# A dense SiLU layer on one core: the first two transposed tiles loaded by two transposes instead of one, and the loads behind them in another order

## The chip, the cores and the metric

The kernel runs on one core of a Trainium2 chip. The metric is the device time of one execution in microseconds (us); less is better. A core has TensorE (matrix products), ScalarE (activations), VectorE, GpSimd and SyncE (SP), each with an instruction stream of its own. SP and ScalarE also issue DMA transfers, and all transfers share the core's 16 DMA engines. Engines wait for each other and for transfers by semaphores.

## The reference

```
B, S, D, F = 1, 2048, 640, 1728            # all bfloat16
h   = einsum("bsd,df->bsf", x, w1)         # 2048 x 640 times 640 x 1728
h   = silu(h)
out = einsum("bsf,fd->bsd", h, w2)         # 2048 x 1728 times 1728 x 640
```

## The kernel before

The first product is computed transposed: `hT` holds the 1728 hidden features on partitions and the 2048 tokens along the free dimension. For that, `x` must be in SBUF with its 640 features on partitions, as five tiles of 128 (`xT[:, k, :]`, k = 0 to 4). The DMA engines transpose `x` on the way in (`turned`, line 90, and line 163). `w1` is kept as `w1s[:, k, :]`, 128 features of tile k by 1728 columns. The hidden features are cut into 13 tiles of 128 columns and a tail of 64. Tokens go in four chunks of 512.

A *step* (line 183) multiplies one 128 x 128 piece of `w1s` with one 128 x 512 piece of `xT`, as two matmuls on the two halves of the array's columns, into one PSUM bank. Elsewhere in the kernel the five steps of a hidden tile stand together. The opening of the first 512 tokens is different, because nothing has been loaded yet: it runs tile by tile over the features. `opening` (line 197) takes k = 0 for the first eight hidden tiles (eight PSUM banks), then k = 1 for the same eight (`sweep`, line 192), then k = 2 and 3; k = 4 follows at line 208 and ends the eight sums, which ScalarE then passes through SiLU (line 179) into `hT`. So each sweep of eight steps needs one *slab* `w1s[:, k, 0:1024]` (256 KB, `slab`, line 118) and one transposed tile `xT[:, k, 0:512]`. Then come the remaining five hidden tiles of the first tokens (lines 222 to 228, which need `ld_rest` and `ld_rest2`), then the three other chunks of tokens (line 229), each after its five transposes `ld_xc[c]`.

The order in which things are loaded is written out by hand. `early` (line 98) moves an instruction into the program's first block, ahead of the barrier that ends it; calls for one engine keep their order. SP's queue in that block is, before:

1. tiles 0 and 1 of the first 512 tokens, one transpose (line 123);
2. the last three hidden tiles of slab 0 (line 148, 96 KB);
3. slab 1, slab 2 (lines 149, 150);
4. tile 2 (line 151), slab 3 (152), tiles 3 and 4 in one transpose (153), slab 4 (154);
5. the columns of `w1` from 1024 on in two loads (lines 156 and 157).

Behind the barrier SP issues the fifteen transposes of the other chunks (line 163) and the loads of `w2` (lines 168 to 171). ScalarE issues one load, the first five hidden tiles of slab 0 (line 124, 160 KB; `NA` = 5), then loads its activation table (line 144).

While the first transfers are under way TensorE multiplies zeros (`dummies`, line 129): thirteen matmuls of 256 columns and a half-width pair (lines 137 and 138). It then waits for tiles 0 and 1 and for ScalarE's part of slab 0 (line 199), and from hidden tile `NA` on for SP's part (line 202).

The second product, from line 247 on, runs after all of this; the change does not touch it. It reads `w2s` and `hT`, and writes the output in blocks of 128 tokens.

Of the kernel before, what the change touches and what calls it, by code (L numbers as in the profile page):

```python
# [9 lines left out]
def bass_standalone__dense_activation_silu__prompt_kernel(  # L10
# [13 lines left out]
    P = 128  # L24
    NB = 8
    BANK = 512
    DT = D // P
    FT = F // P
    FL = F - FT * P
    SCH = 512  # L30
# [10 lines left out]
    with ExitStack() as es:  # L41
# [18 lines left out]
        def sem(name):  # L60
            s = es.enter_context(nc.semaphore(name))
            count[s.name if hasattr(s, "name") else name] = 0
            return [s, 0]

        def tick(ins, s, n=1):
            ins.then_inc(s[0], n)
            s[1] += n
            return (s, s[1])

        def wait(eng, *points):  # L70
            for pt in points:
                if pt is None:
                    continue
                s, v = pt
                key = (id(eng), id(s))
                if seen.get(key, 0) < v:
                    eng.wait_ge(s[0], v)
                    seen[key] = v
# [6 lines left out]
        def load(eng, out_ap, in_ap):  # L85
            s = sem(f"s_ld{n_dma[0]}")
            n_dma[0] += 1
            return tick(eng.dma_start(out=out_ap, in_=in_ap), s, 16)

        def turned(c0, c1, k0, k1):  # L90
            s = sem(f"s_tr{n_dma[0]}")
            n_dma[0] += 1
            return tick(sp.dma_start_transpose(
                out=xT[:, k0:k1, c0:c1], in_=xf[c0:c1, k0 * P:k1 * P]), s, 16)

        ET = mybir.EngineType

        def early(emit, engine, arrived=True):
            n = len(nc.main_func.blocks[0].instructions)
            r = emit()  # L100
            lst = nc.main_func.blocks[0].instructions
            new = lst[n:]
            del lst[n:]
            at = next(
                i for i, ins in enumerate(lst)
                if ins.opcode == ("EventSemaphore" if arrived else "Drain") and ins.engine == engine
            )
            lst[at:at] = new
            return r
# [2 lines left out]
        w2_v = w2[0:F0, :].rearrange("(ft p) d -> p ft d", p=P)  # L112

        NO = NB
        NA = 5
        CO = NO * P

        def slab(eng, k, f0=0, f1=NO):
            return load(eng, w1s[:, k, f0 * P:f1 * P], w1_v[:, k, f0 * P:f1 * P])

        ld_w1 = {}
        ld_t = {}
        ld_t[0] = ld_t[1] = early(lambda: turned(0, SCH, 0, 2), ET.SP, False)
        ld_w1[0] = early(lambda: slab(act, 0, 0, NA), ET.Activation, False)
        p_z = early(lambda: tick(dve.memset(z[:, :], 0.0), s_dve), ET.DVE, False)  # L125

# [2 lines left out]
        def dummies(n, w):  # L129
            for _ in range(n):  # L130
                for c0 in range(0, P, w):
                    pe.matmul(ps[c0:c0 + w, 3, 0:HB], lhsT=z[:, 0:w], rhs=z[:, :],  # L132
                              start=True, stop=True)

        def first_dummies():
            wait(pe, p_z)
            dummies(13, P)
            dummies(1, HC)

        p_warm = early(lambda: tick(pool.memset(warm[:, :], 0.0), s_pool), ET.Pool, False)  # L140
# [4 lines left out]

        early(warm_up, ET.Activation, False)

        ld_w1b = early(lambda: slab(sp, 0, NA, NO), ET.SP, False)
        ld_w1[1] = early(lambda: slab(sp, 1), ET.SP, False)
        ld_w1[2] = early(lambda: slab(sp, 2), ET.SP, False)  # L150
        ld_t[2] = early(lambda: turned(0, SCH, 2, 3), ET.SP, False)
        ld_w1[3] = early(lambda: slab(sp, 3), ET.SP, False)
        ld_t[3] = ld_t[4] = early(lambda: turned(0, SCH, 3, DT), ET.SP, False)
        ld_w1[4] = early(lambda: slab(sp, 4), ET.SP, False)
        CM = CO + 2 * P
        ld_rest = early(lambda: load(sp, w1s[:, :, CO:CM], w1_v[:, :, CO:CM]), ET.SP, False)
# [40 lines left out]
        def opening():  # L197
            first_dummies()
            wait(pe, ld_t[0], ld_w1[0])
            for ft in range(NO):  # L200
                if ft == NA:
                    wait(pe, ld_w1b)
                part(0, ft, 0, SCH, start=True)
            for k in range(1, DT - 1):
                sweep(k, 0, SCH, ld_w1[k], ld_t[k])
# [202 lines left out]
```

## Time and profile before

| | |
|---|---|
| three runs, us | 124.97, 124.90, 124.26; median 124.9 |
| profiled execution, span from first to last instruction | 123.8 us (the page gives no other time for it) |
| TensorE busy | 121.3 us, 98% of the span, 1056 matmuls |
| ScalarE busy | 38.8 us, 31% |
| VectorE busy | 6.9 us, 6% |
| bytes moved | 10.42 MB in 19625 packets |
| SP's DMA issues in the opening | 10, from 0 to 7.7 us |

The span counts from the first instruction that the page counts, here SP's first transpose, to the last. In the timeline each line has the start, the duration, the engine (SPq and ACTq are the DMA issues of SP and ScalarE: the duration is the time that the issue holds the queue, not the transfer), the line of the kernel, the operation, what it writes and reads, how many instructions are merged, and in brackets the idle time before and what ended it. PE is TensorE's matmul, PEld its weight load, which runs ahead of the matmul. The lists of DMA issues have the size and the median time from issue to landing.

### The profile page before, as it was taken

The numbers are of one execution on the slowest core, as the hardware profiler recorded it, in microseconds if no ns is written. First come the engines' busy times: TensorE is split into PE (matmuls) and PEld (weight loads), VectorE is DVE, ScalarE is ACT, GpSimd is POOL, SyncE is SP. The second block draws the span as 40 slices with busy tenths as digits, with TensorE's granted clock in tenths as the row PEclk, the third lists the DMA queues.
The fourth block names the chain that finished last, engine by engine and source line by source line (L and its number), as shares of the span: only waits on it lengthen the run. The fifth ranks groups of instructions, "written<-read, shape, count | busy, mean of one in ns | idle before, by whom it ended". The sixth has DMA issues, their size and how long they took to land.

```text
span 123.8 us, 2298 instructions
## 1 busy us (share of the span) xinstructions
PE 121.3 (98%) x1056; PEld 58.9 (48%) x1057; DVE 6.9 (6%) x11; ACT 38.8 (31%) x67; POOL 0.3 (0%) x5
## 2 busy tenths in 40 slices
PE   8999999999999999999999999999999999999993
PEld 5345545545545545545544444444444444444452
DVE  0000000000000000000000022002200300222001
ACT  4000985555555555555530011001100200110110
POOL 0000000000000000000000000000000000000000
DMA  6999974554894000000000004302200220023112
GB/s 138 239 246 331 138 86 91 100 77 107 214 394 157 0 0 0 3 5 0 0 0 5 0 0 101 74 0 105 107 0 5 106 106 0 5 106 116 53 66 82
DMA packets 19625, 10.42 MB, mean 84 GB/s; under 512 B 13728, under 2 KB 19104, under 8 KB 19616
## 3 DMA queue, kind: packets, MB, share of 16 engines
q1 hardware_dynamic: 19472, 10.11, 34.1%
q10 hardware_dynamic: 144, 0.16, 0.6%
q8 instruction: 8, 0.13, 0.5%
q14 instruction: 1, 0.01, 0.0%
HBM read 4.51 MB, written 2.62 MB: 58 GB/s over the span
## 4 chain that ended last, share of the span: by engine, by line
PE 95%; DMA 3%; ACT 0%; issue 0%
PE ps L175 95%; DMA xT<-in_x_dram 3%; ACT o_sb L256 0%
## 5 line engine op out<-in xcount | busy, mean ns | idle before, releaser
L175 PE MATMUL ps<-xT,w1s 128*64 128x512 bf16 x540 | 59.6, 384 | 0.1
L175 PE MATMUL ps<-w2s,hT 64*128 64x512 bf16 (+3 forms) x376 | 46.0, 369 | 0.2 <-issue 0.2
L175 PEld LDWEIGHTS ps<-xT,w1s 128*64 128x64 bf16 x540 | 30.0, 111 | 29.6 <-issue 1.2
L179 ACT ACTIVATE hT<-ps 128x512 bf16<-128x512 f32 x52 | 30.0, 607 | 29.9 <-PE ps L175 29.9
L175 PEld LDWEIGHTS ps<-w2s,hT 64*128 64x128 bf16 (+1 forms) x377 | 21.0, 95 | 24.2 <-issue 0.2
L256 ACT CAST o_sb<-ps 128x512 bf16<-128x512 f32 (+1 forms) x9 | 5.0, 551 | 41.5 <-PE ps L175 41.5
L175 PE MATMUL ps<-hT,w2s 64*128 64x512 bf16 x104 | 11.7, 376 | 0.0
L175 PEld LDWEIGHTS ps<-hT,w2s 64*128 64x128 bf16 x104 | 5.0, 94 | 6.3 <-issue 0.4
L254 DVE CAST o_sb<-ps 128x512 bf16<-128x512 f32 (+1 forms) x8 | 5.4, 675 | 40.5 <-PE ps L175 40.5
L254 DVE CAST oT<-ps 128x512 bf16<-128x512 f32 x2 | 1.4, 692 | 74.2 <-PE ps L175 74.2
L256 ACT CAST oT<-ps 128x512 bf16<-128x512 f32 x2 | 1.2, 586 | 10.6 <-PE ps L175 10.6
L132 PE MATMUL ps<-z 128*128 128x256 bf16 (+1 forms) x15 | 3.3, 419 | 0.4 <-DVE z L125 0.4
L175 PE MATMUL ps<-w2t,hTt 64*128 64x512 bf16 (+2 forms) x17 | 2.9, 363 | 0.0
L132 PEld LDWEIGHTS ps<-z 128*128 128x128 bf16 (+1 forms) x15 | 1.9, 142 | 1.5 <-issue 0.4
L179 ACT ACTIVATE hTt<-ps 128x512 bf16<-128x512 f32 x2 | 1.2, 598 | 1.0 <-PE ps L175 1.0
L144 ACT ACT_TABLE_LOAD x1 | 1.3, 1283 | 0.5 <-issue 0.5
L175 PEld LDWEIGHTS ps<-w2t,hTt 64*128 64x128 bf16 x17 | 0.9, 94 | 1.1
L175 PE MATMUL ps<-hTt,w2t 64*128 64x512 bf16 x4 | 0.8, 376 | 0.0
L175 PEld LDWEIGHTS ps<-hTt,w2t 64*128 64x128 bf16 x4 | 0.2, 94 | 0.2
L144 ACT ACTIVATE warm<-warm 128x32 f32<-128x32 f32 x1 | 0.2, 229 | 0.0
L125 DVE MEMSET z<- 128x128 uint32 x1 | 0.2, 165 | 0.2 <-issue 0.2
L140 POOL MEMSET warm<- 128x32 f32 x1 | 0.1, 125 | 0.0
(4 smaller groups left out, 0.4 us busy)
## 6 DMA issues: line engine op xcount, KB each, us to landing
out_dram<-o_sb SPq DMA_DIRECT2D x15, 160.0 KB, 1.8
w2s<-in_w_dram SPq DMA_DIRECT2D x1, 1120.0 KB, 6.1
w1s<-in_w_dram SPq DMA_DIRECT2D x4, 256.0 KB, 4.1
w2s<-in_w_dram SPq DMA_DIRECT2D x1, 960.0 KB, 8.2
w1s<-in_w_dram SPq DMA_DIRECT2D x1, 560.0 KB, 7.0
w1s<-in_w_dram SPq DMA_DIRECT2D x1, 320.0 KB, 5.8
xT<-in_x_dram SPq DMA_TRANSPOSE x18, 3.7
w1s<-in_w_dram ACTq DMA_DIRECT2D x1, 160.0 KB, 2.7
```

The lines of the kernel that those rows point to most:

```text
L125: p_z = early(lambda: tick(dve.memset(z[:, :], 0.0), s_dve), ET.DVE, False)
L132: pe.matmul(ps[c0:c0 + w, 3, 0:HB], lhsT=z[:, 0:w], rhs=z[:, :], start=True, stop=True)
L140: p_warm = early(lambda: tick(pool.memset(warm[:, :], 0.0), s_pool), ET.Pool, False)
L144: act.activation(out=warm[:, :], in_=warm[:, :], func=ACT.Silu)
L175: return pe.matmul(o, lhsT=l, rhs=r, start=start, stop=stop, skip_group_check=shared)
L179: r = tick(act.activation(out=out_ap, in_=in_ap, func=ACT.Silu), s_act)
L254: r = tick(dve.tensor_copy(out=out_ap, in_=in_ap), s_dve)
L256: r = tick(act.copy(out=out_ap, in_=in_ap), s_act)
```

## The change

Tiles 0 and 1 of the first 512 tokens are fetched by two transposes of one tile each, issued one after the other by SP; only the first is waited for ahead of the first step, the second ahead of the sweep of k = 1. ScalarE loads four hidden tiles of slab 0 instead of five, and SP loads the other four (128 KB) behind the two transposes. The transpose of tile 2 moves ahead of the load of slab 2. There are twelve full dummies instead of thirteen. The transpose of tiles 3 and 4 is the same, written with 5 for `DT`.

```
         NO = NB
-        NA = 5
+        NA = 4
...
-        ld_t[0] = ld_t[1] = early(lambda: turned(0, SCH, 0, 2), ET.SP, False)
+        ld_t[0] = early(lambda: turned(0, SCH, 0, 1), ET.SP, False)
         ld_w1[0] = early(lambda: slab(act, 0, 0, NA), ET.Activation, False)
...
         def first_dummies():
             wait(pe, p_z)
-            dummies(13, P)
+            dummies(12, P)
             dummies(1, HC)
...
+        ld_t[1] = early(lambda: turned(0, SCH, 1, 2), ET.SP, False)
         ld_w1b = early(lambda: slab(sp, 0, NA, NO), ET.SP, False)
         ld_w1[1] = early(lambda: slab(sp, 1), ET.SP, False)
+        ld_t[2] = early(lambda: turned(0, SCH, 2, 3), ET.SP, False)
         ld_w1[2] = early(lambda: slab(sp, 2), ET.SP, False)
-        ld_t[2] = early(lambda: turned(0, SCH, 2, 3), ET.SP, False)
         ld_w1[3] = early(lambda: slab(sp, 3), ET.SP, False)
-        ld_t[3] = ld_t[4] = early(lambda: turned(0, SCH, 3, DT), ET.SP, False)
+        ld_t[3] = ld_t[4] = early(lambda: turned(0, SCH, 3, 5), ET.SP, False)
         ld_w1[4] = early(lambda: slab(sp, 4), ET.SP, False)
```

More of the change, by code (lines that the diff above doesn't have):

```diff
@@ L114, in bass_standalone__dense_activation_silu__prompt_kernel @@
         NO = NB
-        NA = 5
+        NA = 4
         CO = NO * P
@@ L122, in bass_standalone__dense_activation_silu__prompt_kernel @@
         ld_t = {}
-        ld_t[0] = ld_t[1] = early(lambda: turned(0, SCH, 0, 2), ET.SP, False)
+        ld_t[0] = early(lambda: turned(0, SCH, 0, 1), ET.SP, False)
         ld_w1[0] = early(lambda: slab(act, 0, 0, NA), ET.Activation, False)
@@ L136, in first_dummies @@
             wait(pe, p_z)
-            dummies(13, P)
+            dummies(12, P)
             dummies(1, HC)
@@ L146, in bass_standalone__dense_activation_silu__prompt_kernel @@
         early(warm_up, ET.Activation, False)
+        ld_t[1] = early(lambda: turned(0, SCH, 1, 2), ET.SP, False)
         ld_w1b = early(lambda: slab(sp, 0, NA, NO), ET.SP, False)
         ld_w1[1] = early(lambda: slab(sp, 1), ET.SP, False)
+        ld_t[2] = early(lambda: turned(0, SCH, 2, 3), ET.SP, False)
         ld_w1[2] = early(lambda: slab(sp, 2), ET.SP, False)
-        ld_t[2] = early(lambda: turned(0, SCH, 2, 3), ET.SP, False)
         ld_w1[3] = early(lambda: slab(sp, 3), ET.SP, False)
-        ld_t[3] = ld_t[4] = early(lambda: turned(0, SCH, 3, DT), ET.SP, False)
+        ld_t[3] = ld_t[4] = early(lambda: turned(0, SCH, 3, 5), ET.SP, False)
         ld_w1[4] = early(lambda: slab(sp, 4), ET.SP, False)
```

## The prediction, made before the result was known

> **What bounds the kernel now.** I read the page first, then the chain that ended last, then the timeline of the first 14 us, then the DMA view narrowed to one issue at a time. The page gives TensorE 98% busy, and the chain says what the other 2% are:
>
> ```profile
> by line: PE ps L175 95.3%; DMA xT<-in_x_dram 3.1%; ACT o_sb L256 0.2%; issue 0.2%
> ...
> 0.00 3.78 DMA xT<-in_x_dram
> 3.78 0.04 issue
> 3.82 106.78 PE ps L175 x706
> ```
>
> The end is set by 3.78 us until the first transposed tiles are there, and then by matmuls that never wait. So only two things can move the end: an earlier first real matmul, or a new hole behind it. Both are decided by the order of SP's queue (start, duration, in us):
>
> ```profile
> 0.00 1.33 SPq L93 DMA_TRANSPOSE xT<-in_x_dram  x1
> 0.12 0.37 ACTq L88 DMA_DIRECT2D w1s<-in_w_dram  x1
> ...
> 0.39 3.31 PE L132 MATMUL ps<-z 128*128 128x256 bf16 x15 [0.39 <-DVE z L125]
> ...
> 1.39 1.54 SPq L88 DMA_DIRECT2D w1s<-in_w_dram  x3
> ...
> 2.97 1.16 SPq L93 DMA_TRANSPOSE xT<-in_x_dram  x1
> ...
> 3.82 0.18 PEld L175 LDWEIGHTS ps<-xT,w1s 128*64 128x64 bf16 x4 [0.42 <-DMA xT<-in_x_dram]
> ...
> 5.53 0.18 PEld L175 LDWEIGHTS ps<-xT,w1s 128*64 128x64 bf16 x2 [0.25 <-DMA w1s<-in_w_dram]
> 5.96 0.18 PEld L175 LDWEIGHTS ps<-xT,w1s 128*64 128x64 bf16 x2 [0.25 <-issue]
> 6.30 7.67 PEld L175 LDWEIGHTS ps<-xT,w1s 128*64 128x64 bf16 x72 [0.17 <-issue]
> 8.09 6.44 SPq L163 DMA_TRANSPOSE xT<-in_x_dram  x4
> ```
>
> See three things. SP issues back to back from 0 to 7.7 us: a transpose of one tile holds it 1.16 us, one of two tiles 1.33 or 1.24, so SP's price is nearly per instruction. TensorE's steps (two half-width matmuls) are 0.43 us apart up to about 6 us (5.53 to 5.96) and 0.216 us apart behind it (the 72 weight loads from 6.30 on are 36 steps in 7.7 us); the granted clock column shows 1.00 throughout, so the step spacing is what shows the half pace. And the loads take long from issue to landing, because each waits its turn behind the earlier ones:
>
> ```profile
> w1s<-in_w_dram SPq DMA_DIRECT2D x4, 256.0 KB, 4.1
> ...
> w1s<-in_w_dram SPq DMA_DIRECT2D x1, 320.0 KB, 5.8
> ...
> w1s<-in_w_dram ACTq DMA_DIRECT2D x1, 160.0 KB, 2.7
> ...
> w1s<-in_w_dram SPq DMA_DIRECT2D x1, 96.0 KB, 3.9
> ```
>
> Issue plus landing time, set against the weight load that needs it, gives the slack of each transfer before: rest of slab 0 lands 5.2, needed 5.5; slab 1 5.9 against 6.5; slab 2 6.6 and tile 2 7.2 against 8.2; tiles 3 and 4 9.2 against 10.0; slab 4 10.5 against 11.7; the next weight columns 12.5 against 13.4; the second 512 tokens 18.0 against 18.8. Nothing has much to give.
>
> **Part 1, the start.** Tile 0 alone is half the packets. In the trace those of the first transpose run from 1.7 to 3.25 us, so half of them saves about 0.7: landing at 3.78 - 0.7 = 3.1 (bounds: 2.7, the fastest of the fifteen later one-tile transposes, and 3.8, no gain). Dummies: in the trace one starts 0.21 us after the other (2.71, 2.93) and the half-width pair at 3.28, so with twelve the pair starts at 3.06 and is through at 3.28. The later of 3.1 and 3.28 counts: first real matmul 3.28 instead of 3.82, 0.54 us earlier. All of this lies in the half-pace stretch. If that ends at about 6.15 as now (the step begun at 5.96 is the only one of middle length), 0.54 us there are 0.54/0.43 = 1.27 steps, worth 1.27 x 0.216 = **0.27 us** at the end.
>
> The row has the pace change 5.8 us after the first dummy and 2.3 us after the first real matmul. [...]
>
> **Part 2, SP's queue.** One instruction more: tile 0 (1.25, between 1.16 and 1.33), tile 1 (1.25), then the rest of slab 0. That load goes from 1.39 to about 2.56, slab 1 from 2.00 to 3.15, tile 2 from 2.97 to 3.65, slab 2 from 2.49 to 4.88 (it is also moved past tile 2), slab 3 from 4.17 to 5.4, tiles 3 and 4 from 4.79 to 5.9, slab 4 from 6.07 to 7.2, the two remaining weight loads, the barrier and all fifteen later transposes some 1.2 later. POOL's queue has no DMA in this. ScalarE's load shrinks from 160 to 128 KB; with 2.7 us it lands at 2.8 or sooner, before tile 0, so it costs nothing; ScalarE's first real work is at 12.34.
>
> *Rest of slab 0.* Now needed one step earlier: 3.28 + 4 x 0.427 = 4.99. Bounds for its landing: 2.56 + 1.8 (the 160 KB stores, queue empty) = 4.4; 2.56 + 3.9 (its own row) = 6.4. Before, it landed 1.46 us after the transpose ahead of it; tile 1, issued at 1.31 with the 2.8 of an undisturbed one-tile transpose, lands at 4.1, so I take 4.1 + 1.46 = 5.6. TensorE stands 0.6 us at half pace and goes on with step 4 at 5.6: at 6.15 it has done 4 + 0.55/0.427 = 5.3 steps, before 5.45. So the 0.27 are gone: **+0.04 us** in all. Behind that wait, in order, stands every matmul; ScalarE waits only for their end at 12 us.
>
> *Tile 1* lands by 1.31 + 4.2 = 5.5 at worst; needed 6.5. [...] *Slab 1* lands 0.64 behind the rest of slab 0, as before: 6.2, needed 6.6. Nothing, and 0.4 of cover.
>
> *Slab 2*, moved most, is needed with tile 2 at 8.25 + 0.04 = 8.3. Bounds: 4.88 + 2.7 = 7.6, and 4.88 + 3.9 (the fastest 256 KB load) = 8.8. The row is the nearest thing, but the queue ahead is shorter now (slab 1 and tile 2 only), so 8.5: **+0.25 us**, at full pace, between 0 and 0.5.
>
> *What is late next.* At their old landing times: tiles 3 and 4 5.9 + 4.4 = 10.3 against 10.3 (10.0 + 0.3); slab 4 7.2 + 4.5 = 11.7 against 12.0; next columns 7.8 + 5.8 = 13.6 against 13.7. All fit, none with much. The second 512 tokens: their five transposes were issued 8.09 to 16.45, the last landing 1.6 us behind its issue's end, so SP sets it; 1.2 later is 19.2 against 18.8 + 0.3 = 19.1: **+0.1 us**. Lower end 0: the first two took 1.57 and 2.21 us instead of 1.26, and if they waited for the loads ahead, later issue wins that back; upper end 0.4 if slab 2 is in time. Tokens from 1024 on (24.5 against 32.9) and w2 (39.5 against 61) have room for 1.2 us: nothing, as long as that holds.
>
> **Sum**: 0.04 + 0.25 + 0.1 = +0.4 us on the profiled span of 123.8, hence 124.2. The median of the three runs, 124.9, lies 1.1 above the span; added to that it is 125.3. From the worst ends of these rows (rest of slab 0 at 6.4, resumed at full pace: 0.53 late; slab 2 then hidden under it) comes +0.6 and, with a stretch longer than any row, about +1; from the best ends -0.27. One per cent, 1.25 us, is about what a measurement of this kernel can tell from no change.
>
> **Rivals.**
> 1. *The transfers come in time.* The rest of slab 0 lands by 4.8, slab 2 by 8.2, the second tokens by 18.5. For it: the queue has less waiting in it when those are issued, and two issues behind line 163 held SP 1.3 us longer than needed. Against: the 3.9 to 4.5 of every load in this stretch. Then the earlier start is left: 124.9 - 0.27 = 124.6.
> 2. *The full pace comes later* (slower). The 0.6 us hole at 5.0 us falls into the stretch before the pace changes, and the change waits for unbroken work. For: nothing was that idle before; the hole of 0.33 us ahead of 3.82 did no harm. If the pace changes 2.3 us after work resumes at 5.6, as it did after 3.82, that is 7.9: 1.75 us more at half pace, 0.9 lost; if the whole 5.8 us count starts anew, 11.4, 2.6 lost. The middle, 1.75, hides the 0.35 of later waits: 125.3 + 1.75 - 0.35 = 126.7. It decides once the hole costs the count; from the 0.33 that did not, the point lies above that. [...]
> 3. *A luckier phase* (faster by over 1%). The three runs already differ by 0.7 us, more than my sum; an earlier pace change with all transfers in time would give up to half of the 2.3 us, 1.2: 123.6. Against: transfers then bind sooner, and slacks of 0.3 to 0.8 us eat it.
>
> **Chances.** Forecast 0.56 (its own range 124.7 to 125.9; 0.08 of it, with transfers slower than any row, above 1%); rival 1 0.16; rival 2 0.20; rival 3 0.08. So faster 0.08; within 1% 0.48 + 0.16 = 0.64; slower 0.08 + 0.20 = 0.28. The range from 124.2 to 126.8 leaves out rival 3 and half of rival 2.
>
> **What would show it.** Right: first weight load from xT near 3.3 with no DMA wait; a wait on the w1s load at about 5.0 lasting to 5.6; slab 2's wait near 8.3; SP's first line-163 transpose at 9.3. Rival 1: no w1s wait at all. Rival 2: step spacing of 0.43 beyond 7 us. I am wrong if tile 0 alone lands no sooner than 3.7 (a fixed latency, then the gain is nothing and all waits shift by 0.5), or if a second transpose right behind the first holds SP much less than 1.2 us.

## The result and the profile after

The changed kernel takes 125.70 us in the median of six runs (125.38 to 125.78), the kernel before 124.89 beside it (124.23 to 125.07): a ratio of 1.0087, 95% interval 1.0059 to 1.0114. That is slower by 0.8 us between the medians and by 1.1 us by the ratio, which sets the loss at 0.9%, with an interval that reaches just over 1%. In the experiments below, a loss in us is the ratio's, taken on the median of the kernel before that ran beside it. The profiled execution took 125.70 us with a span of 124.4, so 1.34 us lie around the span; in the profiled executions of the later runs it is 1.32 to 1.37. The ratios leave out runs more than 1.5% above the fastest of the same kernel, which matters in two experiments below (ScalarE with all of slab 0, and with slabs 1 and 3).

Columns of the timeline are as before. This is the changed kernel's matmul stream up to 21 us:

```profile
0.39 3.09 PE L132 MATMUL ps<-z 128*128 128x256 bf16 x14 [0.39 <-DVE z L125]
3.28 1.92 PE L176 MATMUL ps<-xT,w1s 128*64 128x512 bf16 x8
5.45 4.90 PE L176 MATMUL ps<-xT,w1s 128*64 128x512 bf16 x40 [0.25 <-DMA w1s<-in_w_dram]
10.69 10.55 PE L176 MATMUL ps<-xT,w1s 128*64 128x512 bf16 x96 [0.34 <-DMA xT<-in_x_dram]
```

The first real matmul starts at 3.28 instead of 3.82, with no wait ahead of it. Two new holes follow. After four steps TensorE waits for the rest of slab 0 until 5.45: start to start, 0.89 us lie between the fourth and the fifth step instead of 0.43. And ahead of the fourth sweep it waits for tiles 3 and 4: 0.72 us from step to step at 10.69, instead of 0.22. Brackets show less than that, since a matmul is counted until its modelled end, which overlaps the next (0.63 us in the steps 0.43 us apart, 0.38 in those 0.22 apart). The chain that ended last says the same from the other side:

```profile
0.00 1.25 SPq L93
...
1.30 1.24 SPq L93
...
2.59 0.58 SPq L88
...
3.22 0.42 SPq L88
...
3.68 1.12 SPq L93
...
4.85 0.58 SPq L88
...
5.47 0.43 SPq L88
...
5.95 4.61 DMA xT<-in_x_dram
10.55 0.14 issue
10.69 100.45 PE ps L176 x928
```

Before, the chain was one transfer of 3.78 us and then matmuls. Now it runs back to back through seven issues of SP, then through its eighth, the transfer of tiles 3 and 4, and reaches TensorE only at 10.69. What TensorE did before that no longer counts.

Step by step, the ninth step (slab 1) starts within 0.01 us of 6.73 in both profiles, the seventeenth (slab 2) at 8.46, the twenty-fifth (slab 3) at 10.19 before and 10.69 after, and that half microsecond stays: the second 512 tokens start at 19.04 and 19.54. The spans differ by 0.52 us.

### The profile page after: what moved, and what is told of

The parts are those of the page before. It is cut to its first block, busy times and chain, and to the rows that moved or that the text cites. A ratio compares the mean times of both kernels' runs of the same rounds, so it can differ in the third digit from the quotient of the medians.

```text
span 124.4 us, 2298 instructions
## 1 busy us (share of the span) xinstructions
PE 121.4 (98%) x1055; PEld 66.0 (53%) x1056; DVE 7.0 (6%) x11; ACT 38.8 (31%) x67; POOL 0.3 (0%) x5
## 4 chain that ended last, share of the span: by engine, by line
PE 90%; SPq 5%; DMA 4%; issue 1%; ACT 0%
PE ps L176 90%; DMA xT<-in_x_dram 4%; SPq L93 3%; SPq L88 2%; ACT o_sb L257 0%
## 5 line engine op out<-in xcount | busy, mean ns | idle before, releaser
L176 PEld LDWEIGHTS ps<-xT,w1s 128*64 128x64 bf16 x540 | 37.3, 111 | 23.1 <-issue 1.8
```

The lines of the kernel that those rows point to most:

```text
L176: return pe.matmul(o, lhsT=l, rhs=r, start=start, stop=stop, skip_group_check=shared)
```

## The experiments

All ran with the kernel before beside them on the same chip (a place, below). Own times are medians of 6 to 12 runs.

**The second transpose alone.** The kernel before, with tiles 0 and 1 by two transposes and nothing else:

```
-ld_t[0] = ld_t[1] = early(lambda: turned(0, SCH, 0, 2), ET.SP, False)
+ld_t[0] = early(lambda: turned(0, SCH, 0, 1), ET.SP, False)
...
+ld_t[1] = early(lambda: turned(0, SCH, 1, 2), ET.SP, False)
 ld_w1b = early(lambda: slab(sp, 0, NA, NO), ET.SP, False)
```

> The kernel before with one edit: tiles 0 and 1 by two transposes; thirteen dummies, five tiles of slab 0 by ScalarE and the order of the other loads stay. Queue theory (the one more transpose issue holds SP 1.2 us, and the transpose of tiles 3 and 4 behind it lands too late): first real matmul at 3.5, no wait for slab 0 (needed 5.6, lands about 5.3), but the transpose of tiles 3 and 4 is issued at 5.95 as in the changed kernel and lands at about 10.5, so the fourth sweep starts at 10.7: span 124.3 to 124.4, 0.5 us above before. Hole theory (the wait for the rest of slab 0 at half pace costs the time): without that wait it is 0.2 us faster than before, span 123.7.

125.33 us, ratio 1.0061 (1.0036 to 1.0086): 0.76 us slower, most of the loss. Its profile, taken of the slowest of the twelve runs (126.13), has a wait at the fourth sweep (tiles 3 and 4 landing at 10.32), and two that were not expected, for slab 1 and for the second 512 tokens (0.67 us at 19.97):

```profile
3.96 2.31 PE L176 MATMUL ps<-xT,w1s 128*64 128x512 bf16 x16 [0.26 <-DMA xT<-in_x_dram]
6.67 12.83 PE L176 MATMUL ps<-xT,w1s 128*64 128x512 bf16 x114 [0.40 <-DMA w1s<-in_w_dram]
19.97 1.27 PE L176 MATMUL ps<-xT,w1s 128*64 128x512 bf16 x10 [0.47 <-DMA xT<-in_x_dram]
```

The start was missed as well: 3.96 instead of 3.5, since tile 0 alone landed at 3.92, later than tiles 0 and 1 together did before (3.78). The hole theory's 0.2 us faster is out. Fewer dummies, the four tiles and the new place of tile 2 are not needed for a loss of this size.

**The changed kernel with a shorter first hole** (`NA` = 5 again).

> The changed kernel with ScalarE loading five tiles of slab 0 again. Queue theory: the 0.46 us wait for the rest of slab 0 shrinks to under 0.1, TensorE reaches the fourth sweep 0.2 to 0.3 us sooner and stands there that much longer: time as the changed kernel, within 0.15 us. Hole theory: 0.2 to 0.3 us faster than the changed kernel.

125.43 us, ratio 1.0056 (1.0037 to 1.0076); the changed kernel ran at 1.0087, 1.0127 and 1.0069 in three places. The chain of its profile ends exactly as that of the changed kernel:

```profile
5.94 4.36 DMA xT<-in_x_dram
10.30 0.14 issue
10.43 111.82 PE ps L176 x993
```

Its fourth sweep could have started at 9.92 and stood until 10.43, a wait of 0.51 us; in the changed kernel it could have started at 10.19 and stood until 10.69, which is 0.50. So TensorE was sooner by 0.27 us, but it did not wait that much longer: tiles 3 and 4, issued at the same time (5.94 against 5.95), landed 0.25 us sooner. They land between 10.34 and 10.47 from that issue in three later profiles, so such a difference lies within the scatter of this landing, and the two theories can't be told apart by these spans. Nor do the times decide it: the interval overlaps those of the changed kernel in two of its three places. What the chain shows is that this landing sets the end here, and not the first hole, of which 0.36 us are left. All twelve runs lie between 125.18 and 125.79.

**All of slab 0 by ScalarE.** The changed kernel, with SP's part of slab 0 issued by ScalarE behind its own.

```
 ld_w1[0] = early(lambda: slab(act, 0, 0, NA), ET.Activation, False)
+ld_w1b = early(lambda: slab(act, 0, NA, NO), ET.Activation, False)
...
-ld_w1b = early(lambda: slab(sp, 0, NA, NO), ET.SP, False)
```

> The changed kernel with the second half of slab 0 also issued by ScalarE, right behind the first half, so that SP has one load less. Queue theory: all of SP's queue behind it is 0.63 us earlier, slab 0 is complete by about 3.3, tiles 3 and 4 land at about 9.9 instead of 10.55, the fourth sweep starts at about 10.0: span 123.7, about 0.65 us faster than the changed kernel and 0.15 faster than before. Transfer theory (the DMA engines' throughput sets the landing of tiles 3 and 4, whoever issues): tiles 3 and 4 land near 10.4 as before, time within 0.2 us of the changed kernel.

The profile did what the queue theory said: tiles 3 and 4 landed at 9.89, the fourth sweep started at 10.03, span 123.7, own time 125.04. But ScalarE's second load runs beside tile 0, which landed at 4.66 instead of 2.77 (3.40 to 3.92 in the three other profiles from this place, with ScalarE's first load alone beside it), and the twelve runs go from 124.66 to 127.11 in two groups with nothing between 125.41 and 126.28; ratio 1.0058 (1.0020 to 1.0096). One wait was exchanged for another, and something else splits the runs.

**Tiles 3 and 4 ahead of slab 3.**

```
-ld_w1[3] = early(lambda: slab(sp, 3), ET.SP, False)
 ld_t[3] = ld_t[4] = early(lambda: turned(0, SCH, 3, 5), ET.SP, False)
+ld_w1[3] = early(lambda: slab(sp, 3), ET.SP, False)
```

> The changed kernel with the transpose of tiles 3 and 4 ahead of the load of slab 3. Queue theory: the transpose lands at 9.5 to 10.0, but slab 3 is issued 1.3 us later, at 6.75, and with 3.4 us to landing comes at 10.1 to 10.8: the wait ahead of the fourth sweep changes its name from tiles 3 and 4 to slab 3 and stays between 0.2 and 0.8 us; time within 0.4 us of the changed kernel. Transfer theory: tiles 3 and 4 are in first, slab 3 soon behind as the bytes are the same, the wait is as long as before: no difference within 0.1 us.

126.30 us, ratio 1.0120 (1.0086 to 1.0153). The tiles landed at 9.18, slab 3 at 10.77, and the wait changed its name and grew, from 0.50 us to 0.73. The line of its matmul stream:

```profile
10.82 10.55 PE L176 MATMUL ps<-xT,w1s 128*64 128x512 bf16 x96 [0.56 <-DMA w1s<-in_w_dram]
```

**The changed kernel again.**

> The changed kernel itself once more, beside the runs below on one chip. Queue theory: its time is tied to the landing of tiles 3 and 4 (10.3 to 10.6 us whatever the pace did), so its runs lie close together, within 0.5 us, at 125.2 to 125.8, while those of the kernel before spread over 1.2 us (124.0 to 125.2) with the moment at which TensorE's pace doubles. Hole theory: the runs spread as much as before, shifted by 0.8 us.

This went against the queue theory as it stood: 126.37 us, ratio 1.0127 (1.0079 to 1.0174), and the six runs lie from 125.35 to 127.04. The profiled one, 127.04, has no wait at the fourth sweep at all. Its weight loads show why:

```profile
5.76 0.19 PEld L176 LDWEIGHTS ps<-xT,w1s 128*64 128x64 bf16 x4 [1.44 <-DMA w1s<-in_w_dram]
6.19 0.18 PEld L176 LDWEIGHTS ps<-xT,w1s 128*64 128x64 bf16 x2 [0.24 <-issue]
...
9.18 0.18 PEld L176 LDWEIGHTS ps<-xT,w1s 128*64 128x64 bf16 x2 [0.24 <-issue]
9.60 4.50 PEld L176 LDWEIGHTS ps<-xT,w1s 128*64 128x64 bf16 x41 [0.24 <-issue]
```

After the hole (here until 5.76) the steps stay 0.43 us apart until about 9.7. In the first profile they doubled their pace at 6.30. So this is rival 2 of the prediction, in some executions of the same program. The granted clock column reads 1.00 in both profiles, but only because it counts lost clock where the trace has a record of it. The trace of the changed kernel's first profile does hold a record of full clock (1.00), and it begins at 6.29 us, where the steps double their pace; the trace of this run has none.

**Slabs 1 and 3 by ScalarE.** `slab(act, 1)` and `slab(act, 3)` instead of SP's, in the changed kernel.

> The changed kernel with slabs 1 and 3 issued by ScalarE, behind its table load at about 2.05 us; SP has two loads less. Queue theory: the transpose of tiles 3 and 4 is issued at 5.0 (before: 4.79) and lands at 9.2 to 9.6, no wait ahead of the fourth sweep, and the second 512 tokens come at about 18.1: the loss goes, median 124.2 to 124.6, the kernel before within 0.3 us, the changed kernel 0.7 to 1.1 slower. If two transposes in a row, or the half-pace hole, are the cause by themselves, it stays 0.6 us or more slower than before.

Missed. Tiles 3 and 4 were issued at 5.04 and landed at 8.52, and the fourth sweep had no wait; but ScalarE issued both slabs beside its table load, at 0.62 and 1.03 instead of behind it, and they went ahead of what was needed first: tile 0 landed at 3.85, the rest of slab 0 at 6.17, and TensorE stood 1.4 us longer than a step there. 125.25 to 128.16 us in six runs, ratio 1.0115 (1.0068 to 1.0162).

**SP held, nothing else.** The kernel before, with two loads of 8 KB into an unread tile behind the first transpose:

```
+for i in range(2):
+    early(lambda: load(sp, scr[:, 32*i:32*i+32], w1_v[:, 0, 0:32]), ET.SP, False)
 ld_w1b = early(lambda: slab(sp, 0, NA, NO), ET.SP, False)
```

> The kernel before with SP held by two tiny loads (8 KB each into a tile that nothing reads) right behind the transpose of tiles 0 and 1: about 1.05 us more issue time and almost no bytes; nothing else of the change. Queue theory: the transpose of tiles 3 and 4 is issued at 5.85 and lands near 10.3, wait of 0.3 to 0.5 us ahead of the fourth sweep: 0.6 to 1.0 us slower than before, as much as the change itself. If the second transpose, the holes at the start or the dummies are the cause: within 0.2 us of before.

124.92 us, ratio 1.0034 (1.0017 to 1.0051): 0.42 us slower. Holding SP costs time with no second transpose in the kernel, but less than I expected, and in the profile not where I expected it. The next weight load, due at 1.39, came at 2.46, and tiles 3 and 4 were issued at 5.69 and landed at 9.38, earlier than in the changed kernel by more than the issue, and in time: the fourth sweep started at 9.72 without a wait. The chain goes through the held load, the rest of slab 0, which landed at 5.50 and let TensorE stand 0.46 us (the pace had doubled before the first real matmul):

```profile
1.38 0.56 SPq L89
...
2.00 0.42 SPq L89
...
2.46 3.04 DMA w1s<-in_w_dram
5.50 0.04 issue
5.54 115.98 PE ps L178 x1031
```

**Fewer dummies.** The kernel before with `dummies(8, P)`.

> The kernel before with 8 full dummies instead of 13: TensorE stands from 2.4 to 3.8 us, and SP's queue is untouched. If a hole of 1.4 us in the half-pace stretch can put off the doubling of the pace, some runs (a third or more) are 1.2 to 1.8 us slower than the others, as the runs with all of slab 0 by ScalarE fell into two groups 1.5 us apart; the rest lie where the kernel before lies. If holes of that size do nothing, all runs lie within 0.3 us of before.

126.10 us, ratio 1.0124 (1.0089 to 1.0160), 1.5 us slower; all six runs, 125.39 to 126.75, are above the slowest of the kernel before (125.27). Not the two groups that were expected, but clearly a price. The profile has TensorE idle for about 1.1 us ahead of the first real matmul, and the pace doubling near 9.0, after thirteen slow steps:

```profile
2.21 0.13 PEld L132 LDWEIGHTS ps<-z 128*64 128x64 bf16 x2 [0.41 <-issue]
3.55 0.18 PEld L175 LDWEIGHTS ps<-xT,w1s 128*64 128x64 bf16 x4 [1.21 <-DMA xT<-in_x_dram]
...
8.68 0.18 PEld L175 LDWEIGHTS ps<-xT,w1s 128*64 128x64 bf16 x2 [0.25 <-issue]
9.04 4.86 PEld L175 LDWEIGHTS ps<-xT,w1s 128*64 128x64 bf16 x46 [0.18 <-issue]
```

**The hole filled, and the changed kernel a third time beside it.**

```
 if ft == NA:
+    for _ in range(3):
+        pe.matmul(ps[:, 7, 0:HB], lhsT=z[:, 0:P], rhs=z[:, :], start=True, stop=True)
     wait(pe, ld_w1b)
```

> The changed kernel with three more full multiplications of zeros (into the bank of the eighth hidden tile, which its first step overwrites) between the fourth step and the wait for the rest of slab 0, so that TensorE works through the hole; loads and SP's queue as in the changed kernel. Two causes together (a later SP queue, some 0.4 to 0.9 us, and in some runs a doubling of the pace that the hole puts off by 3.4 us, up to 1.6 us more): the second goes, all runs lie within 125.0 to 125.9, median 0.7 to 1.0 us above before, and no profile shows half pace beyond 7 us. If the hole has nothing to do with the late doubling: runs above 126.3 stay, as with the changed kernel.

> The changed kernel again, beside the one with the hole filled. Two causes: runs from 125.3 to 127.1, those above 126.3 with half pace beyond 9 us; median 125.6 to 126.6. One cause (SP's queue alone): all runs within 125.2 to 125.9.

Filled: 125.47 us, 125.31 to 125.79 in eight runs, ratio 1.0059 (1.0038 to 1.0081). Unfilled: 125.57 us, 125.25 to 127.09 in ten runs, ratio 1.0069 (1.0047 to 1.0091); one run, the profiled one, is late, with half pace up to 9.7. The filled kernel's profile is at full pace behind the zeros:

```profile
3.28 1.92 PE L176 MATMUL ps<-xT,w1s 128*64 128x512 bf16 x8
5.12 0.71 PE L204 MATMUL ps<-z 128*128 128x256 bf16 x3
5.76 8.57 PE L176 MATMUL ps<-xT,w1s 128*64 128x512 bf16 x74
```

Over all places, 4 of 22 runs of the changed kernel lie above 126.3 (three of the four in one place), and none of the 20 with the hole filled or shortened by a fifth tile; of 85 runs of the kernel before, none lies above 125.27. The medians of filled and unfilled differ by 0.1 us, less than their intervals. The counts lean the way of rival 2, that a hole at half pace puts the doubling off, and do not prove it; with the kernel of few dummies and the two late profiles beside them I take it as the cause. Why a hole does so in some executions only is not shown.

**A version without the longer queue.** Five tiles by ScalarE; SP issues tile 0, the rest of slab 0, slab 1, then tiles 1 and 2 in one transpose, then slabs 2 and 3, tiles 3 and 4, slab 4.

```
-ld_t[1] = early(lambda: turned(0, SCH, 1, 2), ET.SP, False)
 ld_w1b = early(lambda: slab(sp, 0, NA, NO), ET.SP, False)
 ld_w1[1] = early(lambda: slab(sp, 1), ET.SP, False)
-ld_t[2] = early(lambda: turned(0, SCH, 2, 3), ET.SP, False)
+ld_t[1] = ld_t[2] = early(lambda: turned(0, SCH, 1, 3), ET.SP, False)
```

> A version meant to keep the earlier start without its price: tile 0 alone, then the rest of slab 0 (three tiles, ScalarE loads five), slab 1, then tiles 1 and 2 in one transpose, then slabs 2 and 3, tiles 3 and 4, slab 4: SP has as many issues as before and reaches tiles 3 and 4 at 4.6 (before 4.79); twelve dummies. Queue and hole theory together: first real matmul about 3.3 to 3.5, rest of slab 0 lands at about 4.3 (needed 5.4), no hole, tiles 1 and 2 at 5.9 to 6.4 (needed between 5.7 and 6.45): 0.1 to 0.4 us faster than before, median 124.0 to 124.4. If a transpose split off is harmful by itself, it is 0.4 us or more slower than before.

125.08 us, ratio 1.0029 (1.0006 to 1.0053): better than the change, and still 0.36 us slower than before, where 0.1 to 0.4 us faster was expected. It started at 3.28 and had no hole in the first sweep. Tiles 3 and 4 were issued at 4.80, as before (4.79), and landed at 10.07 instead of 9.24. So the moment of issue does not settle the landing alone: here slab 2 was issued at 3.71, 1.2 us later than before and behind two transposed tiles, and landed at 8.31, slab 3 at 9.01, and the tiles came behind those. In its profile the chain goes through slab 2, ahead of which TensorE stood 0.26 us; at the fourth sweep it stood 0.10.

```profile
2.41 1.25 SPq L93
...
3.71 4.61 DMA w1s<-in_w_dram
...
8.36 102.29 PE ps L175 x944
```

**SP held right ahead of tiles 3 and 4.** The kernel before with four tiny loads there; all that is issued earlier is untouched.

> The kernel before with SP held by four tiny loads (8 KB each, into a tile that nothing reads) right ahead of the transpose of tiles 3 and 4, about 1.85 us of issue time; everything issued earlier is untouched. Queue theory (the moment at which SP issues that transpose sets its landing, and from there on the end): it is issued at 6.65 and lands at 10.6 to 11.1, the fourth sweep waits until then: 0.9 to 1.4 us slower than before. Transfer theory (its landing is set by the backlog of transfers ahead of it, which here is not longer than before): it lands by 10.2, at most 0.4 us slower.

125.48 us, ratio 1.0082 (1.0050 to 1.0115), 1.0 us slower: the queue theory's size, and a late issue of these tiles and of what stands behind them is enough for it. The landing was sooner than that theory said, 9.99 from an issue at 6.66, as the transfer theory had it: with slab 3 landing at 7.61 and otherwise only the tiny loads ahead, the transfer takes 3.3 us, where it took 4.6 in the changed kernel. So the moment of issue and what waits ahead both set the landing. In this profile the second 512 tokens are waited for as well, 0.14 us. The wait at the fourth sweep, and where it ended:

```profile
5.09 4.29 PE L178 MATMUL ps<-xT,w1s 128*64 128x512 bf16 x38 [0.21 <-DMA w1s<-in_w_dram]
10.13 4.08 PE L178 MATMUL ps<-xT,w1s 128*64 128x512 bf16 x36 [0.75 <-DMA xT<-in_x_dram]
```

**What stays open.** Holding SP by 1.07 us at the same place costs 0.42 us (0.2 to 0.6); the second transpose alone, the change with five tiles and the change with the hole filled cost 0.7 to 0.8 (intervals from 0.45 to 1.1), and the change itself 1.1 by the ratio of the first six runs (0.7 to 1.4), none of them late. How much of the difference is the 0.26 us by which tiles 3 and 4 are issued later still, and how much the order of what is ahead of them, was not separated. Nor is it always the same transfer that comes late: by the chains it is tiles 3 and 4 in the changed kernel's first profile, with five tiles and with SP held right ahead of them, but slab 3 where that was moved behind them, the rest of slab 0 with SP held early and in both late profiles, slab 2 in the version with tiles 1 and 2 in one transpose, and the second 512 tokens with the second transpose alone. That a later queue on SP costs time is shown; which of its transfers pays is known for the profiled executions only. None of the versions beats the kernel before.

## Why the prediction was right, and where it was not

The forecast was 125.3 with a range of 124.2 to 126.8 and 0.64 for within 1%; measured 125.7, +0.8 us. The mechanism was right in its main line (an earlier start that the half pace and the first late load give back, then a later queue on SP that costs some tenths), but the term that made the loss was put at nothing, and that the span's sum came out near (+0.4 against +0.52) is luck: two of its three terms, 0.35 of the 0.4 us, cost nothing.

- *The start.* Right: 3.28. Tile 0 landed at 2.77, not 3.1, and the dummies set the start, as they do in two of the three profiles of this kernel; in the third tile 0 set it, at 3.29. The landing of a single tile is no fixed quantity, though: with the second transpose alone it was 3.92, and with tiles 3 and 4 ahead 3.71, the value from which on the prediction calls itself wrong.
- *What the earlier start is worth.* The 0.27 us of 0.54 take it that the pace changes at about 6.15, as before; that it stays there was an assumption, and other profiles have it from before 3.6 to 9.71 (the last section). Right for this profile: the pace doubled at 6.30, and the ninth step began at 6.73 in both kernels, so that the earlier start was gone by then (predicted 0.04 us behind).
- *Rest of slab 0.* Right in place and size: landed 5.40 (5.6 predicted), hole of 0.46 us (0.6). In the two later profiles 5.72 and 5.83.
- *Slab 2.* Wrong: +0.25 was put there and it cost nothing. It landed at 8.22 against the 8.3 needed, 3.4 us after its issue and not the 3.6 taken. The margin is thin: with the hole filled it landed at 8.42 and TensorE stood 0.09 us.
- *Tiles 3 and 4.* Wrong the other way: "10.3 against 10.3 ... all fit". They landed at 10.55, 4.6 us after their issue and not the 4.4 taken, and the sweep could have started at 10.19, as before, since slab 2 had not held TensorE back. This one term is +0.50 us, in place of +0.25 for slab 2 and +0.1 for the second tokens, which landed at 18.61 and were not waited for.
- *The sum.* +0.4 on the span was predicted, +0.52 measured. The rest, up to +0.8 in the medians, comes with the step from span to median: I added 1.1 us to 123.8. With the 1.34 us of the other runs the profiled execution of the kernel before took about 125.2, just above its 124.2 to 125.1. Its pace doubled late, near 6.1. In executions where it doubles early the kernel before should gain, and its runs go down to 124.0; the changed kernel cannot, because tiles 3 and 4 hold it (125.25 at best in 22 runs). No early execution of the kernel before was profiled, so this is inferred; the five-tile version shows the second half of it, with the pace doubled before 4.6 and the fourth sweep still waiting until 10.43. Rival 3 named that mechanism, and the sum left it out.
- *Rival 2* does occur, it seems, in 4 of 22 runs of the change (two of them profiled, with the late doubling), at 1.2 to 1.5 us above the median of its other runs (125.6). It was not in the six of the result. Its size was taken at 1.75 less what it hides, 1.4, which is near.
- *Rival 1* is out: no profile of the changed kernel has the transfers in time.
- *What can be told.* The prediction takes 1% as about the least that a measurement of this kernel can tell from no change; the intervals here are 0.2 to 0.5% to either side, and a loss of 0.3% was told from none.

## What to carry to other kernels

Where a queue issues back to back and its transfers have slack of a few tenths, one more issue at its head moves every issue behind it (here by 1.16 to 1.30 us, up to the first transpose of the later tokens, for those that kept their place), and a late transfer among these sets the end. The landings do not all move by the same amount: here those issued about 1.2 us later, in the same order as before, landed between 0.3 us sooner and 1.3 later. So write down, for each transfer, when it lands and when it is needed, with a range, and expect the loss at any whose range crosses its need, even if another was moved more. A start that comes earlier while the work behind it is limited by arrivals is given back at the first late arrival (here 0.54 us, gone by the ninth step). A single profile is one draw of when the pace doubles (6.30 and 9.71 us in two profiles of the changed kernel); before adding a span's difference to a median, see whether the profiled execution stands at the top or the bottom of its kernel's runs.

## What the runs showed of the hardware that I had not expected

The doubling of TensorE's pace moves between executions of one program. In profiles without a long hole it came between before 3.6 us (the run with SP held ahead of tiles 3 and 4 has its first real steps at full pace) and 6.3 us; with holes of 0.5 to 0.9 us (0.46, 0.77 and 0.88) behind the fourth step, at 6.30, about 9.7 and about 9.7 in three profiles of one kernel. The two late ones (9.60 and 9.71) are 3.3 and 3.4 us behind the early one. That distance lies between different executions, and no run shows what sets it.

Two of the fourteen traces hold a record of full clock: from 6.29 us in the changed kernel's first profile and from 5.59 with the hole filled, each time where the pace doubles. The others have none, and none covers the half pace of the start, so there the spacing of the steps has to be read and not the clock column. A hole behind the doubling did not bring half pace back: with slabs 1 and 3 by ScalarE, TensorE stood 1.4 us after four steps at full pace and went on at 0.25 and 0.21 us a step.

A transposed tile's landing varies much, from place to place as well as with what runs beside it: tile 0 alone landed at 2.77, 2.81 and 3.24 in three profiles of the changed kernel, at 3.40, 3.71 and 3.92 in three versions that ran in another place, with one load of ScalarE of 128 or 160 KB beside it as in these, and at 4.66 there with a second load of ScalarE beside it.
